# One core, a mixer kernel from a written-out order of 638 tasks: a new order on every engine

## The chip, the cores and the metric

The kernel runs on one core of a Trainium2 chip. The metric is the time of one execution on the device, in microseconds. The five engines are called by the names that the profile uses: PE (matrix products), DVE (vector), ACT (activation functions), POOL and SP. SP does no arithmetic here and only issues transfers; ACT and POOL issue a few as well.

## What is computed

```python
xn = _layernorm(x)                      # x: 1 x 2048 x 448
s = _A_ref(xn, ...)                     # h[t] = Lam_bar * h[t-1] + B_bar xn[t];  y = 2 Re(C h) + xn * Dskip
g = _silu(_B_ref(xn, ...))              # _layernorm, w1 (448 x 1792) + b1, gelu, w2 (1792 x 448) + b2
return x + s * g
```

The recurrence has 448 complex states with diagonal `Lam_bar = exp(dt * Lam)`. All inputs and the output are bf16.

## The kernel before

The 2048 rows are cut into four groups g of 512 rows, each group into two blocks b of 256 rows, each block into its even and odd rows (par 0 and 1), so that a tile has 128 partitions of 448 elements. The stages of a group are:

- the two layernorms at once: statistics of x (L378, for group 0 L399), scale factors (`ln_scale`, L440 to L450), and the application that writes `xn_sb` (for the recurrence) and `xn2_sb` (for the MLP; both show as `xn_sb` in the profile, L464 and L465, for group 0 L419);
- transposes of both to `xnT` and `xn2T`, for group 0's MLP operand on PE with copies by ACT and DVE (L422, L390), for all others by DMA transposes that SP issues (L83);
- the first MLP product, `mm1` (L741 and L742), seven pairs j of feature tiles, each in two phases, with a GELU on ACT for each pair (L745); a pair holds two PSUM banks until its GELU has read them, so that pair j=5 of a group can begin only after the GELU of pair j=2;
- the second, `mm2` (L760 and L762), with a bias addition on DVE (L763, it reads `b2bc`), a tanh on ACT (L764) and a gate on DVE (L765);
- the recurrence: `bu` (L669), a rotation and two scans on DVE (`ssm`, L684 to L715), and the output product `ym` (L793 to L799), after which DVE multiplies by the gate and adds the skip terms (L802, L805).

Tables are computed once from the parameters: sines on ACT into `WT` (L599; these need their own activation table, which is loaded before them, and GELU's table is loaded again after them, L604), products `LB` from B (`combine`, L619 to L622, an ACT or DVE half that writes `tmp` and a DVE half), their transposes `BT`, and `CQ`, `CZ` from C. `M0` (L658 to L660) is a product of these tables. The skip vector `dbc` and the bias `b2bc` are loaded by POOL, `dbc` only after `b2bc` has landed (L356 and L357); `dbc` is then halved by one small instruction (L359).

Nothing of the order is left to a scheduler at run time. The program adds 638 tasks, each with an engine, its instructions, and the names it reads and writes. `link` derives the dependences from the names in the order in which tasks were added. `ORDER` (L152) lists the task numbers in the order of issue, so that each engine gets its own tasks in the order in which the list names them, and `SECOND` (L171) lists the tasks, of those added with two possible engines, that run on the second one. Within an engine a waiting task holds up all that stand behind it; this holds for SP's queue of transfers too.

```python
        for k in SECOND:
            self.tasks[k].choose(1)
        order = [self.tasks[k] for k in ORDER]
...
        for t in order:
            eng, seen = self.engs[t.eng], self.seen[t.eng]
...
            for sem, val in need.items():
                if seen.get(sem, 0) < val:
                    eng.wait_ge(self.sems[sem], val)
                    seen[sem] = val
```

In the order before, SP loads block 1 of x first, then the even and the odd rows of block 0, then the pieces of w1, x of group 1, w2, C and B. The first DMA transpose in SP's queue is one of C (`Cr<-vs`, L83), which waits for the loads of C; behind it stand the two transposes `xn2T` of group 1's MLP operand, then x of group 2, and the transposes of group 0's `xnT`, of C and of B. PE runs 28 products on `ident` alone at the start (L829), which fill time only.

Of the kernel before, what the change touches and what calls it, by code (L numbers as in the profile page):

```python
# [149 lines left out]


ORDER = [int(k) for k in """  # L152
# [17 lines left out]
""".split()]  # L170
SECOND = [int(k) for k in """  # L171
23 34 45 65 66 73 75 78 80 82 84 85 89 100 132 156 158 160 184 186 191 195 219 221 225 241 245 247 248 257 261 265 267 323 324 325 326 334 346 355 363
374 375 385 396 400 402 443 444 446 469 483 484 501 503 504 506 507 508 509 515 517 528 532 533 616 632
""".split()]


# [748 lines left out]
```

## Time and profile before

| what | us |
|---|---|
| median of 3 runs (lowest to highest) | 158.9 (158.78 to 159.37) |
| profiled execution | 160.4 |
| its span, first to last instruction | 158.7 |
| PE busy | 148.0 (93%) |
| DVE busy | 136.2 (86%) |
| ACT busy | 96.6 (61%) |
| POOL busy | 38.9 (25%) |

The granted clock is 1.000 over the span. All times in a trace are counted from the span's start. Records of one engine overlap a little where one instruction follows another without a wait, so that their durations add up to more than the busy time; PE's overlap most, and for PE the distance from one group's start to the next's is used.

### The profile page before, as it was taken

How to read it: one execution, taken by the hardware profiler on the slowest of the kernel's cores; microseconds unless marked ns; L12 is line 12 of the kernel's file. 1: busy time of each engine (PE TensorE's matmuls, PEld its weight loads, DVE VectorE, ACT ScalarE, POOL GpSimd, SP SyncE). 2: the span in 40 equal slices, each digit the busy share in tenths (PEclk: the TensorE clock that was granted, in tenths of full speed). 3: DMA queues.
4: the chain of work that ended last, by engine and by line, in shares of the span. 5: the costliest groups of instructions: out<-in, count | busy, mean ns of one | idle time of the engine just before them, and what ended most of it. 6: DMA issues, size and time to landing. Idle time of an engine off the chain costs nothing.

```text
span 158.7 us, 3107 instructions
## 1 busy us (share of the span) xinstructions
PE 148.0 (93%) x1130; PEld 88.2 (56%) x1130; DVE 136.2 (86%) x295; ACT 96.6 (61%) x180; POOL 38.9 (25%) x94
## 2 busy tenths in 40 slices
PE   0989999499989999999999999999999999999992
PEld 0977755154446656665564555676444665555552
DVE  1789998379699799999899799857899978999794
ACT  3598978997599767597989251231484767035110
POOL 5628623030902000036000008450000260001231
PEclk9999999999999999999999999999999999999999
DMA  4999967999997450000000335310940000000103
GB/s 110 271 302 281 326 183 141 166 222 244 136 173 147 65 99 0 0 2 0 4 0 0 66 62 99 100 40 1 94 145 0 0 4 0 0 31 27 62 2 116
DMA packets 31238, 14.75 MB, mean 93 GB/s; under 512 B 24752, under 2 KB 30774, under 8 KB 31222
## 3 DMA queue, kind: packets, MB, share of 16 engines
q1 hardware_dynamic: 30912, 14.26, 41.7%
q0 software_dynamic: 160, 0.23, 1.0%
q8 instruction: 9, 0.15, 0.4%
q10 hardware_dynamic: 150, 0.05, 0.1%
q14 instruction: 7, 0.06, 0.1%
HBM read 6.89 MB, written 1.84 MB: 55 GB/s over the span
## 4 chain that ended last, share of the span: by engine, by line
PE 70%; DMA 14%; SPq 9%; DVE 2%; issue 2%; ACT 1%; DVEq 0%
PE psum L760 20%; PE psum L741 15%; PE psum L669 14%; PE psum L793 12%; DMA Bn<-in_A_B_im_dram 7%; SPq L84 7%; PE psum L796 4%; DMA x_all<-in_A_x_dram 4%; PE psum L658 3%; DMA xnT<-xn_sb 3%; SPq L83 2%; PE psum L799 1%; DVE lnst L378 1%; ACT gT L745 1%; ACT xn_sb L465 0%
## 5 line engine op out<-in xcount | busy, mean ns | idle before, releaser
L741 PE MATMUL psum<-xn2T,w_sb 64*128 64x512 bf16 (+1 forms) x462 | 45.5, 345 | 3.4 <-DMA xn2T<-xn_sb 2.4
L760 PE MATMUL psum<-w_sb,gT 128*128 128x448 bf16 x224 | 44.5, 353 | 0.0
L745 ACT ACTIVATE gT<-psum,b1f 128x512 bf16<-128x512 f32 (+1 forms) x66 | 36.1, 621 | 6.0 <-PE psum L741 5.6
L741 PEld LDWEIGHTS psum<-xn2T,w_sb 64*128 64x128 bf16 x462 | 25.5, 109 | 21.4 <-issue 5.3
L760 PEld LDWEIGHTS psum<-w_sb,gT 128*128 128x128 bf16 x224 | 21.6, 98 | 20.4 <-issue 0.6
L669 PE MATMUL psum<-xnT,BT 128*128 128x256 bf16 x196 | 24.1, 273 | 0.5 <-issue 0.5
L669 PEld LDWEIGHTS psum<-xnT,BT 128*128 128x128 bf16 x196 | 18.6, 98 | 6.5 <-issue 1.6
L390 ACT ACTIVATE u_sb<-psum 128x512 bf16<-128x512 f32 (+2 forms) x21 | 9.9, 470 | 14.1 <-PE psum L669 14.0
L764 ACT ACTIVATE th<-o 128x448 f32<-128x448 f32 x16 | 9.1, 576 | 9.7 <-DVE o L763 9.6
L390 ACT ACTIVATE vs<-s_w 64x256 bf16<-64x256 f32 (+2 forms) x14 | 7.9, 565 | 11.5 <-DVE s_w L695 7.5
L777 POOL TENSOR_TENSOR xr<-xd,g_sb 128x448 f32<-128x448 bf16 x4 | 4.8, 1194 | 41.1 <-DVE tmp L805 23.2
L693 DVE TENSOR_TENSOR_SCAN s_w<-dk,vs 128x774 f32<-128x774 f32 x8 | 13.9, 1758 | 0.0
L465 ACT ACTIVATE xn_sb<-x_all,lnw 128x448 bf16<-128x448 bf16 (+2 forms) x18 | 11.4, 672 | 3.9 <-POOL xd L777 2.2
L802 DVE TENSOR_TENSOR t<-psum,g_sb 128x448 bf16<-128x448 f32 (+2 forms) x17 | 10.0, 591 | 4.3 <-PE psum L796 2.3
L704 POOL TENSOR_TENSOR ang<-s_w,ang 128x16 f32<-128x16 f32 x3 | 2.0, 677 | 40.3 <-ACT s_w L702 20.7
L793 PE MATMUL psum<-CZ,h_sb 128*128 128x448 bf16 x56 | 11.9, 353 | 0.0
L763 DVE TENSOR_TENSOR o<-psum,b2bc 128x448 f32<-128x448 f32 x16 | 9.8, 615 | 1.0 <-PE psum L760 1.0
L765 DVE SCALAR_TENSOR_TENSOR g_sb<-th,o 128x448 bf16<-128x448 f32 x16 | 10.4, 650 | 0.2 <-ACT th L764 0.2
L793 PE MATMUL psum<-CQ,h_sb 128*128 128x448 bf16 (+2 forms) x54 | 10.5, 332 | 0.0
L378 DVE BATCH_NORM_STATS2 lnst<-x_all 128x6 f32<-128x448 bf16 x12 | 7.3, 619 | 1.4 <-DMA x_all<-in_A_x_dram 1.4
L619 ACT ACTIVATE tmp<-Cr,cw 128x448 f32<-128x448 bf16 (+1 forms) x10 | 6.5, 664 | 2.6 <-DVE CZ L622 1.3
L793 PEld LDWEIGHTS psum<-CZ,h_sb 128*128 128x128 bf16 x56 | 5.4, 98 | 4.9 <-DVE o L763 0.4
(161 smaller groups left out, 193.8 us busy)
## 6 DMA issues: line engine op xcount, KB each, us to landing
out_dram<-tmp SPq DMA_DIRECT2D x7, 224.0 KB, 1.9
x_all<-in_A_x_dram SPq DMA_DIRECT2D x3, 448.0 KB, 5.7
w_sb<-in_B_w_dram SPq DMA_DIRECT2D x3, 448.0 KB, 8.5
w_sb<-in_B_w_dram SPq DMA_DIRECT2D x3, 384.0 KB, 5.2
vs<-in_A_C_re_dram SPq DMA_DIRECT2D x1, 392.0 KB, 7.6
vs<-in_A_C_im_dram SPq DMA_DIRECT2D x1, 336.0 KB, 10.7
Bn<-in_A_B_re_dram SPq DMA_DIRECT2D x1, 336.0 KB, 11.0
Bn<-in_A_B_im_dram SPq DMA_DIRECT2D x1, 336.0 KB, 11.6
```

The lines of the kernel that those rows point to most:

```text
L84: return e.dma_start(out_ap, in_ap)
L390: kb.either(("act", [lambda e, o=o, i=i: e.activation(o, i, ACT.Copy) for o, i in pairs]), ("dve", [lambda e, o=o, i=i: e.tensor_copy(o, i ...
L465: ("act", [lambda e, o=o, i=i: e.activation(o, i, ACT.Identity, bias=nb, scale=rs) for o, i in parts], 0.75, 0.2)]
L669: fns = [lambda e, r=r, m=m, d=d: e.matmul(psum[:, 4, r * NK:(r + 1) * NK], BT[:, m, d, :], xnT[:, gx, d, :], start=(d == 0), stop=(d == 6 ...
L693: dve(lambda e, so=so, vi=vi: e.tensor_tensor_scan(so, dk[:].rearrange("p i c -> p (i c)"), vi, 0.0, ALU.mult, ALU.add), ["v", "vl", "dk", ...
L741: return lambda e: e.matmul(view(bk[k]), w1_sb[rows, d, fcol(2 * j + k)], rhs[rows, d, :, :], start=not second and n == 0, stop=second and ...
L745: act([lambda e, k=k: e.activation(gT[:, gb, 2 * j + k, :].rearrange("p (r c) -> p r c", r=2)[:, :, cols], view(bk[k]), ACT.Gelu_apprx_tan ...
L760: fns = [lambda e, fi=fi: e.matmul(psum[:, bk, 0:D], gT[:, gb, fi, q * 128:(q + 1) * 128], w2_sb[:, fi, :], start=(fi == 0), stop=(fi == N ...
L763: dve(lambda e: e.tensor_tensor(o2[:, fb, :], psum[:, bk, 0:D], b2bc[:], ALU.add), [f"ps{bk}", "b2bc"], [f"oo{fb}"], 0.62, prio - 76)
L765: dve(lambda e: e.scalar_tensor_tensor(out=g_sb[:, gs, :], in0=th[:, fb, :], scalar=1.0, in1=o2[:, fb, :], op0=ALU.add, op1=ALU.mult), [f" ...
L793: fns = [lambda e, k=k: e.matmul(psum[:, bk, c0:c1], h_sb[:, hb, k, k0:k0 + 128], cm[:, k, c0:c1], start=(k == 0), stop=False) for k in ra ...
L802: dve(lambda e: e.tensor_tensor(t3[:, fb, c0:c1], psum[:, bk, c0:c1], g_sb[:, gs, c0:c1], ALU.mult), [f"ps{bk}", f"g{gs}"], [f"t3{fb}_{c0} ...
```

## The change

Only the two lists change. The 638 tasks, what each computes, and the dependences between them stay. 77 of the tasks that may run on either of two engines now run on the other one: 25 go from DVE to POOL, 14 from DVE to ACT, 24 from ACT to DVE, 14 from POOL to DVE. PE and SP keep their 128 and 59 tasks. The places that matter below (a place is the position in the engine's own queue):

| task | what | before | after |
|---|---|---|---|
| 20, 18, 19 | loads of x: block 1, block 0 even rows, block 0 odd rows | SP 1st, 2nd, 3rd | SP 3rd, 2nd, 1st |
| 1, 90 | `ident` finished; the 28 filling products | POOL behind the b1 loads; PE behind the parameters | POOL ahead of the b1 loads; PE first |
| 213 | first transpose of C | SP 23rd | SP 29th |
| 260, 263 | `xn2T` transposes of group 1 | SP 24th, 25th | SP 21st, 22nd |
| 203 | load of the real part of C | SP 12th | SP 23rd, behind 263 |
| 257 | scale factors of group 1 | DVE | POOL, directly ahead of 43 |
| 43, 44 | loads of `b2bc` and `dbc` | POOL 30th, 41st | POOL 22nd, 27th |
| 259 | application, group 1, block 0, odd rows | DVE | ACT |
| 45 | halving of `dbc` | DVE | ACT 29th, ahead of the sines |
| 189 | `tmp` for the first `LB` | DVE | ACT 30th, ahead of the sines |
| 190 | first `LB` | DVE 59th | DVE 57th, behind both bias additions of group 0's block 0 |
| 278 | `mm2` of group 0, block 1, even rows | PE behind five phases of group 1's `mm1` | PE ahead of all of group 1's `mm1` |
| 315, 461, 457 | three `mm2` of groups 1 and 2 | PE 65th, 87th, 103rd | PE 83rd, 111th, 115th |
| 630, 634 | the last two output pieces | 256 columns, then 192 | 192 columns first; last addition on DVE |

The first lines of both lists, old and new:

```diff
 ORDER = [int(k) for k in """
-13 20 0 16 9 24 15 18 17 19 4 25 21 22 1 26 14 124 30 91 27 47 90 48 125 49 50 29 92 94 2 93 51 46 54 66 52 55 95 97 32 53 96 122 57 23 203 105 98 58
-101 99 205 123 106 100 102 103 126 5 104 33 56 39 108 107 40 112 130 42 28 114 59 65 113 127 41 109 60 154 38 111 110 128 204 131 129 115 35 117 37
-116 31 118 132 120 168 34 3 252 133 119 61 67 251 62 140 69 121 68 135 256 160 70 250 155 8 71 12 72 134 74 73 136 170 6 249 139 43 144 75 255 169 167
...
+0 5 16 19 13 9 1 90 24 15 25 18 94 14 95 20 91 4 21 92 105 22 26 17 96 47 101 124 93 27 97 122 102 48 65 106 23 125 99 29 50 98 30 100 123 2 49 51 54
+52 104 55 103 3 108 66 56 126 46 28 107 112 113 109 8 111 114 127 110 128 130 131 32 53 31 170 132 167 57 250 33 251 249 34 115 67 42 6 58 129 41 59
+117 140 116 118 10 133 254 40 168 252 119 120 121 135 144 139 134 136 255 256 253 12 39 141 137 60 257 145 142 43 169 154 62 7 171 258 149 146 63 74
...
 SECOND = [int(k) for k in """
-23 34 45 65 66 73 75 78 80 82 84 85 89 100 132 156 158 160 184 186 191 195 219 221 225 241 245 247 248 257 261 265 267 323 324 325 326 334 346 355 363
-374 375 385 396 400 402 443 444 446 469 483 484 501 503 504 506 507 508 509 515 517 528 532 533 616 632
+52 62 65 66 67 69 74 76 83 85 89 100 106 132 155 156 159 163 176 183 184 187 189 219 223 225 229 235 239 241 243 245 248 259 261 326 340 353 377 378
+396 443 444 447 468 469 480 481 484 500 506 508 510 513 528 636
```

28 rows, old and new, of the table ORDER are left out of this document.

## The prediction

> **What bounds the kernel now.** I read the page's chain first, then busy time by stretches cut at PE's own waits, then the timelines of the engines around those waits.
>
> ```profile
> PE 70%; DMA 14%; SPq 9%; DVE 2%; issue 2%; ACT 1%; DVEq 0%
> ```
>
> The chain that ended last is PE for 70% of the span. So every microsecond in which PE has nothing to do counts, and the stretches say where these are (columns: stretch, length, then busy time of PE, PEld, DVE, ACT, POOL).
>
> ```profile
> 0.79:9.06 8.27, 4.67 (x58) 4.40 (x59) 4.75 (x18) 4.25 (x12) 4.33 (x17) 1.00 0.86 216
> 9.06:20.98 11.92, 11.86 (x177) 9.33 (x178) 10.99 (x52) 10.98 (x23) 7.31 (x31) 1.00 1.09 307
> 20.98:29.08 8.10, 8.10 (x43) 4.00 (x42) 6.96 (x20) 6.40 (x12) 1.71 (x5) 1.00 0.83 132
> 29.08:31.45 2.37, 0.00 (x1) 0.03 (x1) 0.69 (x1) 2.36 (x3) 0.00 (x0) 1.00 0.75 184
> 31.45:45.23 13.78, 12.96 (x105) 6.54 (x105) 11.35 (x32) 10.93 (x19) 5.50 (x13) 1.00 1.17 201
> 45.23:155.19 109.96, 109.86 (x747) 63.58 (x748) 100.09 (x171) 61.70 (x115) 19.14 (x24) 1.00 0.21 42
> 155.19:158.70 3.51, 0.56 (x7) 0.34 (x5) 1.36 (x4) 0.00 (x0) 0.75 (x1) 1.00 0.39 131
> ```
>
> The first `mm1` begins at 9.06 (PE's busy time before it is mostly the 2.98 us of filling products). Then PE idles 2.37 us in one piece, 0.8 us up to 45.23, 0.1 us in the next 110 us, and it is done 3.5 us before the end. An order can move only these: 9.06, 2.37, 0.8 and 3.5. No PE instruction goes away.
>
> The 2.37 us are a wait for group 1's `xn2T`:
>
> ```profile
> 31.45 3.86 PE L741 MATMUL psum<-xn2T,w_sb 64*128 64x512 bf16 x34 [2.37 <-DMA xn2T<-xn_sb]
> ```
>
> and SP's queue shows why it was late: the transpose of C stands in front (22.56, it waits for C's loads), and a load of 448 KB right behind.
>
> ```profile
> 22.56 1.59 SPq L83 DMA_TRANSPOSE Cr<-vs  x1
> 24.20 2.68 SPq L83 DMA_TRANSPOSE xn2T<-xn_sb  x2
> 26.93 0.72 SPq L84 DMA_DIRECT2D x_all<-in_A_x_dram  x1
> ```
>
> **Start.** Before, block 0's odd rows were the third load; DVE's statistics on them began at 5.43, and the chain statistics, Ln and Exp, application (7.01), transpose (7.82), copy on ACT (8.25 to 8.85) led to 9.06. Loaded first, the odd rows should land 2.4 to 3.0 us after 0.79 (rows of the 112 KB loads), so this part ends two microseconds earlier. But DVE's new queue has block 1's first statistics ahead of the application of block 0's even rows, and block 1, now third, lands at about 5.4. From there: statistics 0.54, application to 6.4, transpose to 7.1, then DVE must do block 1's second statistics, the b1 copy and the w1 copy (moved to it from ACT) before the last copy, 7.4 to 7.8. `mm1` starts near 7.9. Block 1's own factors (1.54 us on DVE) then begin at about 8.2, just where they were (8.09), but the two applications follow sooner; its transposes come at about 10.5 where they were at 11.36. From there PE is full to 20.98. I take **-0.8**; the ends are -0.2 (the factors decide alone) and -1.1.
>
> **The wait for `xn2T` goes: -2.37.** Group 1's scale factors, 20.28 before, are on POOL now: 3.5 us (row of group 2's, 39.33 to 42.87) after the sine's 3.2 us, which I place at 11.5 to 14.7; so 18.3. The applications, two of four on ACT behind group 0's GELUs, end near 21 and 23, and SP issues the transposes at about 21.5 and 23 instead of 24.20 and 25.54. Moreover `mm2` of 278 (2.65 us) now stands ahead of group 1's `mm1`. PE asks for `xn2T` at 31.0: 20.2 plus 8.1 plus 2.65. Even with the 5.8 us that the second transpose took before, it is there by 29.
>
> **What is late next: the GELUs of group 1.** ACT's new queue has, behind group 0's last GELU (about 25), the halving of `dbc`, then `tmp` of the first `LB`, then the sine stage. The halving was on DVE at 33.16 with nobody behind it in a hurry; now ACT stands until `dbc` has landed. POOL issues `dbc` only when `b2bc` has landed, and `b2bc` only behind the scale factors, at 18.3 instead of 16.24. Both landings have rows:
>
> ```profile
> b2bc<-in_B_b_dram POOLq DMA_DIRECT2D x1, 112.0 KB, 6.5
> dbc<-in_A_Dskip_dram POOLq DMA_DIRECT2D x1, 112.0 KB, 5.3
> ```
>
> The smallest POOL loads took 2.9 and 3.4. I take 5.0 for `b2bc` (fewer loads are ahead of it than at 16.24) and 5.2 for `dbc`: landing at 28.5, between 24.1 (twice 2.9) and 31.3 (twice 6.5). Then ACT needs: halving 0.6 (no row; 0.26 on DVE below, 0.76 for an ACT application of that size above), `tmp` 0.6, and the sine stage,
>
> ```profile
> 26.92 1.28 ACT L599 ACT_TABLE_LOAD   x1
> 28.21 1.72 ACT L599 ACTIVATE WT<-s_w 128x768 bf16<-128x768 f32 x2
> 29.84 0.65 ACT L619 ACTIVATE tmp<-Bn,cw 128x448 f32<-128x448 bf16 x1
> 30.40 2.21 ACT L599 ACTIVATE WT<-s_w,sgn 128x1024 bf16<-128x1024 f32 x3
> 32.69 1.28 ACT L604 ACT_TABLE_LOAD   x1
> ```
>
> from 26.92 to 33.97 less the `tmp` in it, 6.5; then a tanh 0.5 and the first pair of GELUs 1.1: 9.3, so 37.8. PE reaches pair j=5, which needs these banks, at 31.0 plus five phases 3.8 plus one 0.85, 35.6. It waits 2.2, and 0.5 more for j=3, whose GELU pair ends 1.17 later: **+2.7**. The same wait holds `LB` on DVE (190 needs that `tmp`), hence `BT` and `bu`.
>
> [...]
>
> **The rest.** The 0.8 us of small idle: BT's transposes still come one per 1.3 us from SP and follow `LB`; I keep 0.5, **-0.3**. In the 110 full microseconds DVE's records give up 18.7 us and take 15.8 (by the rows of the forms they become), so its load is not higher; the three late `mm2` fill PE between `ym` pieces. I set it at 0, between 0 and +2. Tail: before, the last 192 columns waited for DVE until 156.38 and their load-out was issued at 156.78; now these are finished first, and the last piece ends with a multiplication 0.43 and an addition (0.75 on POOL before, some 0.4 on DVE): **-0.5**, ends 0 and -0.7.
>
> **Sum** against the span of 158.7: -0.8 -2.37 +2.7 -0.3 +0 -0.5 = -1.3. The profiled execution took 160.4, 1.7 outside the span; the median of the runs shown is 158.9, from which the same -1.3 gives **157.6**.
>
> **Rivals.**
> - *POOL's loads land early.* If `dbc` is there by 26.3, the GELUs are no later than PE and the 2.7 go: 154.9. For: fewer transfers run at 18 to 25. Against: both rows above.
> - *`dbc` lands late and ACT's wait outweighs all.* Slower than before from a landing after 29.8, by over 0.5% after 30.6. With scale factors one microsecond later and 6.5 for each load: 32.3, so 161.4. For: the load's packets moved only at 21 to 22, five microseconds after 16.24, and the same POOL operation (L578, 128x128) took 0.49 in one place and 0.65 in another. [...]
> - *Handovers between DVE and PE.* DVE's queue is strict, and PE now meets it closely: the bias addition behind 315, the second `ym` of each block waiting for the multiplication that frees its bank, `CZ` for the first `ym`. Five such waits of 0.4 (the size of the small waits at 43.9 and 45.2) make 2: 159.4 or so.
> - *Nothing net:* the new wait equals all gains, 158.9.
>
> **How the numbers follow.** Forecast 157.6 with its own range 156.9 to 158.1: 0.42. Early loads 154.9: 0.15. Late `dbc` 161.4: 0.20. Handovers 159.4: 0.15. Nothing net: 0.08. A measurement of this kernel can tell about 0.5%, 0.8 us. Faster 0.57, within 0.23, slower 0.20. The range goes from 154.9 to 160.2: all but the far part of the late case.
>
> **What would show it.** `mm1` near 7.9; no wait for `xn2T`; a wait of ACT for `dbc`, ending near 28.5, and one of PE for GELUs of 2 to 3 us at 36 to 39. Without ACT's wait the sum is wrong by 2.7. If PE idles by more than 1 us in sum after 45, DVE's handovers were mis-sized.

## The result and the profile after

The changed kernel takes 163.7 us (median of 4, 163.14 to 165.81), the kernel before 159.1 beside it: **1.027 times as long**, interval 1.022 to 1.032. The forecast was 157.6, so not only the size but the sign was wrong.

The first profiled execution of the changed kernel took 165.8 us, with the granted clock at 0.979: it fell to half in two stretches of 3.4 us. So the times below are from a second profiled execution of the same kernel (after_again, below): 164.8 us, span 163.0, clock 1.000, against 160.4 and 158.7 before.

The page's chain now reads as follows. It was PE for 70% before, and DVE for 2%.

```profile
DVE 48%; PE 25%; DMA 10%; issue 6%; POOL 5%; SPq 2%; ACT 2%; DVEq 0%; POOLq 0%; ACTq 0%
```

Busy time by stretches of after_again, cut at the start of `mm1`, the end of group 0's `mm1`, PE's wait for GELUs at 38, the first `bu` and PE's end (columns as before: stretch, length, PE, PEld, DVE, ACT, POOL, then the granted clock, the DMA engines' share and GB/s):

```profile
9.09:22.63 13.54, 13.54 (x177) 10.58 (x178) 10.37 (x44) 10.24 (x23) 7.82 (x22) 1.00 0.81 242
22.63:37.99 15.36, 15.36 (x99) 7.67 (x98) 12.49 (x29) 12.06 (x21) 6.37 (x19) 1.00 0.89 155
37.99:39.08 1.09, 0.00 (x1) 0.01 (x2) 1.09 (x3) 1.09 (x3) 0.96 (x4) 1.00 1.00 196
39.08:43.47 4.39, 3.98 (x34) 2.16 (x35) 3.86 (x11) 4.12 (x8) 0.00 (x0) 1.00 0.96 114
43.47:159.44 115.97, 112.65 (x767) 64.64 (x765) 107.81 (x181) 58.11 (x108) 33.80 (x47) 1.00 0.23 51
159.44:163.00 3.56, 0.00 (x0) 0.00 (x0) 1.56 (x5) 0.00 (x0) 0.57 (x1) 1.00 0.38 129
```

The wait for `xn2T` is gone. But the 177 products and transposes of group 0's `mm1`, which took 11.92 us, take 13.54; PE waits 1.1 us at 38; PE is idle for 3.3 us of the long stretch, where it was 0.1; DVE is busy for 93% of it, where it was 91%; and the tail is 3.56 instead of 2.91 (from PE's last product). What PE waits for, from the view of waits (total, times, longest); of the first row 1.5 us lie at 38 to 40.3, before the long stretch:

```profile
PE psum L741 <- ACT gT L745: 2.0, 3, 1.1
...
PE psum L793 <- DVE t L802: 1.4, 1, 1.4
PE psum L669 <- ACT u_sb L390: 1.0, 1, 1.0
```

Between the two profiled executions the span grew by 4.3 us: group 0's `mm1` +1.6, PE's waits behind it +1.4 (3.2 to 4.6), the tail +0.65, and the rest in waits below 0.2 us and in the interleaving of PE's work. The first of these terms belongs to these two executions: over the profiles of all runs, group 0's `mm1` ends at 20.4 to 22.7 with the start of the changed kernel (nine profiles, the middle one 21.6) and at 21.0 to 23.2 with that of the kernel before (seven, the middle one 21.5).

### The profile page after: what moved, and what is told of

The parts are those of the page before. It is cut to its first block, busy times and chain, and to the rows that moved or that the text cites. A ratio compares the mean times of both kernels' runs of the same rounds, so it can differ in the third digit from the quotient of the medians.

```text
span 164.1 us, 3109 instructions
## 1 busy us (share of the span) xinstructions
PE 151.4 (92%) x1130; PEld 89.2 (54%) x1130; DVE 142.5 (87%) x285; ACT 89.8 (55%) x168; POOL 54.0 (33%) x111
## 4 chain that ended last, share of the span: by engine, by line
DVE 43%; PE 28%; ACT 8%; DMA 7%; issue 6%; POOL 5%; DVEq 0%; ACTq 0%; POOLq 0%
PE psum L741 14%; DVE s_w L693 5%; PE psum L793 5%; DVE t L802 4%; DVE tmp L805 4%; DVE g_sb L765 4%; DVE lnst L378 3%; PE psum L760 3%; DMA dbc<-in_A_Dskip_dram 3%; PE psum L669 3%; ACT WT L599 2%; POOL lnw L442 2%; DMA dk<-in_B_b_dram 2%; DVE o L763 2%; DVE CZ L622 2%
## 5 line engine op out<-in xcount | busy, mean ns | idle before, releaser
L741 PE MATMUL psum<-xn2T,w_sb 64*128 64x512 bf16 (+1 forms) x462 | 48.1, 363 | 3.0 <-ACT gT L745 2.5
L741 PEld LDWEIGHTS psum<-xn2T,w_sb 64*128 64x128 bf16 x462 | 26.9, 112 | 22.9 <-issue 4.8
L390 ACT ACTIVATE u_sb<-psum 128x512 bf16<-128x512 f32 (+2 forms) x20 | 10.0, 498 | 22.3 <-PE psum L669 22.2
L777 POOL TENSOR_TENSOR xr<-xd,g_sb 128x448 f32<-128x448 bf16 x6 | 6.9, 1153 | 24.8 <-DVE g_sb L765 15.6
L802 DVE TENSOR_TENSOR t<-psum,g_sb 128x448 bf16<-128x448 f32 (+2 forms) x17 | 9.9, 593 | 3.9 <-PE psum L796 3.0
L464 DVE TENSOR_SCALAR xn_sb<-x_all,lnw 128x448 bf16<-128x448 bf16 (+2 forms) x25 | 10.7, 452 | 1.7 <-ACT xn_sb L465 0.8
L465 ACT ACTIVATE xn_sb<-x_all,lnw 128x448 bf16<-128x448 bf16 (+2 forms) x15 | 9.0, 646 | 3.4 <-POOL lnw L444 3.3
L765 DVE SCALAR_TENSOR_TENSOR g_sb<-th,o 128x448 bf16<-128x448 f32 x16 | 9.7, 619 | 1.1 <-ACT th L764 1.1
L777 POOL TENSOR_TENSOR xr<-x_all,xr 128x448 f32<-128x448 bf16 x6 | 7.6, 1259 | 5.1 <-DVE xr L778 4.9
L704 POOL TENSOR_TENSOR ang<-s_w,ang 128x16 f32<-128x16 f32 x2 | 0.5, 242 | 25.6 <-ACT s_w L702 25.6
```

The lines of the kernel that those rows point to most:

```text
L390: kb.either(("act", [lambda e, o=o, i=i: e.activation(o, i, ACT.Copy) for o, i in pairs]), ("dve", [lambda e, o=o, i=i: e.tensor_copy(o, i ...
L464: on = [("dve", [lambda e, o=o, i=i: e.tensor_scalar(o, i, rs, nb, op0=ALU.mult, op1=ALU.add) for o, i in parts], 0.4, 0.12), ("act", [lam ...
L741: return lambda e: e.matmul(view(bk[k]), w1_sb[rows, d, fcol(2 * j + k)], rhs[rows, d, :, :], start=not second and n == 0, stop=second and ...
L765: dve(lambda e: e.scalar_tensor_tensor(out=g_sb[:, gs, :], in0=th[:, fb, :], scalar=1.0, in1=o2[:, fb, :], op0=ALU.add, op1=ALU.mult), [f" ...
L777: kb.either(("pool", lambda e, o=o, i0=i0, i1=i1, op=op: e.tensor_tensor(o, i0, i1, op), 1.37, 0.15), ("dve", lambda e, o=o, i0=i0, i1=i1, ...
L802: dve(lambda e: e.tensor_tensor(t3[:, fb, c0:c1], psum[:, bk, c0:c1], g_sb[:, gs, c0:c1], ALU.mult), [f"ps{bk}", f"g{gs}"], [f"t3{fb}_{c0} ...
```

## The experiments

All are compared with runs of the kernel before on the same chip (159.4 to 159.6 us). Theory G: the late `dbc` and the wait for GELUs is what the change lost. Theory D: DVE has become the bound after 45 us, stretched by POOL's work. A third, the clock theory, came with the first profiles.

| run | us | ratio to before, interval |
|---|---|---|
| old45_new | 163.5 | 1.023, 1.018 to 1.029 |
| new45_old | 168.4 | 1.057, 1.053 to 1.062 |
| bias_early | 164.8 | 1.036, 1.031 to 1.041 |
| skips_dve | 165.2 | 1.037, 1.033 to 1.042 |
| after_again | 164.1 | 1.030, 1.025 to 1.035 |
| fill42 | 164.6 | 1.029, 1.023 to 1.035 |
| pool_tiny | 160.5 | 1.007, 1.004 to 1.010 |
| before_xt | 163.1 | 1.023, 1.017 to 1.028 |
| before_tiny | 161.5 | 1.013, 1.008 to 1.019 |
| after_act | 171.6 | 1.079, 1.073 to 1.085 |
| act_start | 171.0 | 1.075, 1.069 to 1.080 |
| before_xt2 | 159.6 | 1.002, 0.998 to 1.005 |
| stats_cut | 162.9 | 1.022, 1.018 to 1.026 |
| before_double | 164.2 | 1.028, 1.024 to 1.032 |
| tiny_start | 158.1 | 0.993, 0.990 to 0.997 |
| before_xt3 | 159.7 | 1.001, 0.998 to 1.003 |
| gelu_early | 163.2 | 1.024, 1.018 to 1.030 |
| gelu_fill | 161.2 | 1.011, 1.005 to 1.017 |

### Halves of the two orders

```diff
-ORDER = NEW
+ORDER = OLD[:280] + [k for k in NEW if k not in OLD[:280]]
```

> Every engine follows the old order for what it issues up to about 45 us and the new one from there, with the new choice of engines for that part. Theory G (the late dbc, PE's wait for GELUs at 37, is what the change lost, and the rest only hands it on): nothing of it is in this kernel, so about the time before, 158.5 to 159.5. Theory D (DVE has become the bound after 45: in the changed kernel's profile it has 104.8 us of work left after 50 us, before 96.8, and its operations that run beside POOL's are stretched by 8.8 us in sum, before 3.1): 161 to 162.5, with PE waiting for DVE or ACT between 60 and 115.

```diff
-ORDER = NEW
+ORDER = NEW[:270] + [k for k in OLD if k not in NEW[:270]]
```

> The other half: every engine follows the new order up to about 45 us and the old one from there. Theory G: PE's wait for GELUs (2.0 us in the profiled execution, 3.7 where the clock is not lowered before it) is in this kernel, no wait for xn2T; 161.5 to 163. Theory D: the gains of the start and of xn2T against that wait leave about +1, 159.5 to 160.5.

(`SECOND` follows the order in each part.) The first is slow, by 1 us more than D's range allowed, with the 1.4 us wait for L802 at 110 and no loss ahead of 45. The second is slower than either order and than both expectations: PE waits 5.7 us at 53.3 for ACT's copy of `u_sb`, a wait that neither order has. A joint of two orders makes waits of its own, so these two say only that the late part is slow by itself.

### The filling products and the clock

```diff
-... start=True, stop=True) for _ in range(28)],
+... start=True, stop=True) for _ in range(42)],
```

> The changed kernel itself, on the chip of the three that follow, for a base to compare them with and for another profile of it. 163 to 164.5. If DVE is what bounds it after 45, its profile shows PE waiting again near 65, 81 and 111, whatever the clock at 8 and at 39 did.

> The changed kernel with 42 filling products instead of 28, so that PE is busy from 1.7 to about 6.4 instead of to 4.9. Clock theory (the filling products end too early, PE stands 1.5 us, and the next 3.4 us run at half rate): the first 14 mm1 products should take 0.33 to 0.45 us a phase again instead of 0.6 to 0.85, and PE should be 1.5 us further at 12 us. At the end: -1.5 if PE bounds what follows; about 0 to -0.4 if PE only asks earlier for the GELUs at 35 to 39 and later for DVE (theory D).

PE's timeline at the start of after_again,

```profile
1.74 3.17 PE L829 MATMUL psum<-ident 128*128 128x128 bf16 x28 [1.74 <-POOL ident L298]
...
9.09 4.35 PE L741 MATMUL psum<-xn2T,w_sb 64*128 64x256 bf16 x40 [0.19 <-DVE cw L529]
```

and of fill42:

```profile
1.73 3.81 PE L829 MATMUL psum<-ident 128*128 128x128 bf16 x42 [1.73 <-POOL ident L298]
...
8.40 2.38 PE L741 MATMUL psum<-xn2T,w_sb 64*128 64x256 bf16 x40 [0.48 <-DVE cw L529]
```

28 filling products take 3.17 us, one per 0.107 us in the trace. The 42 take 3.81, because from 4.5 us on there is one per 0.056. So PE begins at half rate here, and when it goes to full rate differs: 2.8 us after its first product in fill42, and in gelu_fill not within the 4.66 us that the same 42 take there. In after_again the filling ends at half rate, PE then waits 1.5 us for the bias columns, and the same 40 products of `mm1` take 4.35 us instead of 2.38. The granted clock reads 1.00 in both (each microsecond from 9 to 13); the spacing of the products is what shows it. In the changed kernel's first profile it went another way: PE was at full rate at 6.8 (four of the transposes in 0.40 us, 0.61 in after_again), and the granted clock was 0.50 from 8.4 to 11.8. With 28 products in the new place these 40 take from 2.38 (after_act) to 4.35 us in nine profiles, with 42 always 2.38 (four profiles). In that first profile the half clock lasted 3.4 us both times (8.4 to 11.8, 39.1 to 42.5). What decides between the rates no run here shows.

fill42 is 2.2 us further at the end of group 0's `mm1` (20.41 against 22.56, the starts of `mm2`) and in the median not faster at the end: PE reaches the GELUs sooner, waits there for 1.4 and 0.4 us, and then the clock is at 0.50 from 38.6 to 42.0, so that 28 products take 4.90 us (3.22 in after_again):

```profile
38.53 4.90 PE L741 MATMUL psum<-xn2T,w_sb 64*128 64x512 bf16 x28 [0.41 <-ACT gT L745]
```

Four of its six executions have a mean clock of 0.985 to 0.987 like this one; the two at 1.000 took 162.6 and 162.9 us, over 1 us less than after_again. So what the added products gained was lost again to the wait and, in most executions, to the clock behind it.

### The wait for the GELUs

In these and the next, POOL's queue is shown as task numbers.

```diff
-12 60 257 43 7 63 64 158 44
+12 43 60 44 257 7 63 64 158
```

> The changed kernel with b2bc's load moved in POOL's queue to 10.6 us (where POOL has nothing to do) and dbc's load ahead of group 1's scale factors. dbc should land near 22 instead of 29.1, ACT should not wait for it, and the GELU that PE waits for should end near 35.3 instead of 39.0. Theory G: the wait goes and the time with it, 160 to 160.5. Theory D: PE asks earlier and waits later for DVE instead; no more than 1.5 us of it shows at the end, 162.2 to 163.5.

It did not test what it was to test: `b2bc`, issued at 12.4, took 6.8 us in the crowd of the first loads (347 GB/s in that slice of the page), POOL stood 2.7 us for it ahead of group 1's scale factors, and what stood behind them came 2 to 3 us later. So the factors go first:

```diff
-12 60 257 43 7 63 64 158 44
+12 43 60 257 44 7 63 64 158
```

> The changed kernel with b2bc's load as soon as POOL is free for it (about 12.5) and dbc's right behind group 1's scale factors; nothing is left out. bias_early tried this and failed to test it, since POOL waited for b2bc ahead of the scale factors and all behind them came 3 us late; here the factors go first. ACT should not wait for dbc, and the GELUs that PE waits for at 37 to 39 should end 2 us sooner or more (36.3 in tiny_start). Theory G: PE's wait falls below 0.5 us and 1.5 to 3 us come back, 161 to 162.5. Theory D: the wait goes and little shows at the end, 163 to 164.5.

> gelu_early with 42 filling products: both losses ahead of 45 us undone, the skip products whole and beside DVE as in the changed kernel. tiny_start, the same with cut skip products, took 158.1. Theory D: 161.5 to 163.5, some 4 to 5 us above tiny_start, with PE waiting near 65, 81 and 111. If the losses ahead of 45 us were the cause: 158.5 to 160.5.

In gelu_early `dbc` lands at 24.9 and ACT doesn't wait; PE's waits for GELUs fall from 2.0 to 0.5 us (a new one of 0.5 for a transpose of `BT` follows), and 0.6% come back, 1.0 us (the two intervals, 1.018 to 1.030 and 1.025 to 1.035, overlap). Both losses ahead of 45 undone (gelu_fill) bring 1.9%, 3.0 us, though the filling products alone brought nothing. Neither loss shows fully while the other is there: PE that is early waits for the GELUs, and GELUs that are early wait for a late PE. In gelu_fill the mean clock is 0.996 or more in every execution, so what fill42 lost to the clock is not lost there. Theory D alone expected 161.5 or more, theory G alone 160.5 or less; 161.2 lies between them, nearer to D.

### POOL's skip products beside DVE

```diff
-SECOND = NEW_SECOND
+SECOND = NEW_SECOND + {247 323 324 325 363 507 509 616}
```

> The changed kernel with the eight skip products that went from DVE to POOL (1.0 to 1.7 us each there, 0.38 to 0.62 on DVE before) back on DVE, at the same places of the order. Theory G: they lie beside other work, 163.2 to 164.2. Theory D in the form that POOL's work stretches DVE's: 4.5 us come back to DVE and about as much stretching goes, 162 to 164, with the stretched DVE operations at 60 to 63 and at 136 back to 0.4 to 0.95 us. If it is clearly slower than 164.2, the moves to POOL were worth more than the stretching they cost.

```diff
-... ("pool", lambda ...: e.tensor_tensor(o, i0, i1, op), ...)
+... ("pool", lambda ...: e.tensor_tensor(o[:, 0:8], i0[:, 0:8], i1[:, 0:8], op), ...)
```

> The changed kernel with every skip product on POOL (L777) cut to 8 of its 448 columns, so the output lacks most of the skip term in those places; all waits stay, and POOL's busy time falls from 54 to about 33 us. Theory D with stretching (DVE's operations beside POOL's take 8.8 us longer in sum, most of it beside these products): DVE's busy time falls by 4 to 5 us, the wait at 111 (1.4 us) goes, the end comes 2.5 to 4 us earlier, 160 to 161. If the stretching is only beside the point, 163 to 164.

(pool_tiny, before_tiny and tiny_start also clear `xd` and `xr` once, 1.7 us on POOL in its idle time.) DVE's timeline of after_again ahead of PE's longest wait for DVE,

```profile
107.00 1.31 DVE L464 TENSOR_SCALAR xn_sb<-x_all,lnw 128x384 bf16<-128x384 bf16 x2
108.23 0.61 DVE L805 TENSOR_TENSOR tmp<-t,xr 128x448 bf16<-128x448 bf16 x1
108.77 1.78 DVE L685 TENSOR_TENSOR pb<-u_sb,WT 128x1536 bf16<-128x1536 bf16 x1
110.48 0.38 DVE L805 TENSOR_TENSOR tmp<-t,x_all 128x448 bf16<-128x448 bf16 x1
110.89 0.62 DVE L802 TENSOR_TENSOR t<-psum,g_sb 128x448 bf16<-128x448 f32 x1
```

POOL's at the same time,

```profile
107.11 1.15 POOL L777 TENSOR_TENSOR xr<-xd,g_sb 128x448 f32<-128x448 bf16 x1
108.34 1.40 POOL L777 TENSOR_TENSOR xd<-xn_sb,dbc 128x448 bf16<-128x448 bf16 x1
109.69 0.94 POOL L709 COPY h_sb<-h_sb 128x7 bf16<-128x7 bf16 x1
```

and DVE's in pool_tiny, where those products are cut:

```profile
104.93 0.60 DVE L464 TENSOR_SCALAR xn_sb<-x_all,lnw 128x384 bf16<-128x384 bf16 x2
105.45 0.62 DVE L805 TENSOR_TENSOR tmp<-t,xr 128x448 bf16<-128x448 bf16 x1
105.98 0.95 DVE L685 TENSOR_TENSOR pb<-u_sb,WT 128x1536 bf16<-128x1536 bf16 x1
```

The same two DVE rows take 1.31 and 1.78 us beside POOL, 0.60 and 0.95 without, and POOL's small copy (0.21 before) takes 0.94. The 1.5 us in these two rows is what makes the multiplication of L802 late, for which PE stands 1.38 us; in pool_tiny that wait is not there. From the first `bu` to PE's last product, PE is idle for 0.06 us in pool_tiny (length less PE's busy time), where it was 3.3 in after_again and 0.1 before:

```profile
43.70:155.74 112.04, 111.98 (x767) 65.03 (x765) 100.98 (x183) 58.09 (x108) 18.98 (x43) 1.00 0.23 54
```

It is not that POOL's products themselves are late: in after_again neither DVE, ACT nor PE waits for one. Over the whole kernel, the DVE operations that overlap POOL's are 8.4 us longer than their own kind elsewhere (before 3.1, pool_tiny 1.8), and the cut gives back 3.6 us. Moving the eight tasks back to DVE (skips_dve) halves the stretching to 4.3 but gives DVE its work again: DVE is busy for 142.1 us, as in the changed kernel, and nothing is won (165.2 against 164.1 us, with overlapping intervals).

L802, which reads PSUM, keeps its length: its two at 156.19 take 1.15 us together beside a POOL product of 1.11, and in the first profile its operations on 448 columns take at most 0.63 each, the six beside POOL's work as well. So in these rows L685 and L464 are held up and L802 is not. POOL's products are stretched too: the one at 108.34, which began 0.11 us behind a DVE addition (L805, 0.61 as elsewhere), took 1.40, where the one at 29.89 took 1.03. Why some operations are held up and others not is not shown.

Two controls (before_tiny with pool_tiny's edit on the kernel before), and the opposite experiment on the kernel before:

> A control for the cut skip products: the kernel before with every skip product on POOL cut to 8 of 448 columns (most of the skip term is lacking where POOL computes it). There DVE's operations beside POOL's are stretched by 3.1 us in sum, and PE has 0.1 us of idle time from 45 on. Theory D: PE bounds this kernel, so what DVE gets back is not worth anything: 158.5 to 159.5, against -3.6 us in the changed kernel. If cut skip products make any kernel faster (fewer waits on POOL), it gains 1.5 us or more here as well.

```diff
-e.bn_stats(lnst[:, q, :], x_all[:, 2 * g + b, par, :])
+e.bn_stats(lnst[:, q, :], x_all[:, 2 * g + b, par, 0:(D if g < 2 else 16)])
```

> The changed kernel with the eight statistics of groups 2 and 3 (L378 on DVE, 0.61 us each) taken over 16 of 448 columns, so the layernorm of half of the rows is not the reference's. Order, queues and POOL's work stay; DVE has some 3.7 us less to do between 51 and 90 us. If DVE is the bound there, 1.5 to 3.5 us come back: 160.5 to 162.5. If it is not, and only POOL's products themselves were late in pool_tiny: 163.5 to 164.5.

```diff
-("pool", lambda ...: e.tensor_tensor(o, i0, i1, op), ...)
+("pool", [lambda ...: e.tensor_tensor(o, i0, i1, op)] * 2, ...)
```

> The kernel before with each of its eleven skip products on POOL done twice (where that product adds x, x is added twice). POOL gets some 12 us more, still under 35% busy. Stretching: about half of a POOL product's length is added to DVE's operations beside it, so DVE's sum of stretching goes from 3.1 to 6 or more, and the time, where DVE has little room left, by 1 to 4 us: 160.5 to 163. If POOL beside DVE costs nothing in this order: 159 to 160.

before_tiny missed its range: in its profile PE stayed at half rate until 13.3, and group 0's `mm1` ended at 23.2 instead of 20.98, so its sum is no clean control; three of its six executions also have a mean clock of 0.987 to 0.989. From the first `bu` to the end it takes 113.5 us, the kernel before 113.4; pool_tiny takes 115.1 there and after_again 119.5 (in the changed order 14 products of `mm1`, 1.6 us, lie behind the first `bu` that lay ahead of it before). So the cut is worth 4.4 us in the changed order and nothing in the old one. stats_cut takes 3.5 us off DVE's busy time with POOL untouched and is 0.8%, 1.3 us, faster than after_again, between its two ranges and with intervals that just touch: DVE's work counts there, at about a third of its length. before_double shows the same from the other side: added POOL work alone, in the old order, takes DVE from 136.2 to 142.2 busy, the stretching from 3.1 to 9.2, PE's idle time behind the first `bu` from 0.1 to 3.1,

```profile
42.96:157.32 114.36, 111.30 (x751) 63.52 (x751) 106.40 (x176) 61.31 (x115) 32.56 (x37) 1.00 0.20 41
```

and the time to 1.028, which is what the whole change did and more than its range. A part of that is waiting for the longer products themselves (DVE stands 0.9 us at 96.2 for one, ACT 5.5 for another, 2.2 before), so of the two the cut is the cleaner experiment.

tiny_start has the edits of pool_tiny, fill42 and gelu_early:

> pool_tiny (skip products on POOL cut to 8 columns, 160.5) with 42 filling products and b2bc loaded at about 12 and dbc right behind group 1's scale factors, which should bring dbc to about 25.5 instead of 29 and the GELUs 3 us forward. If the changed kernel's gains at the start were hidden behind DVE, they should show now that DVE has room: 157.5 to 159. If the order loses them again in any case (another wait between 45 and 110), 160 to 161.

0.993 (0.990 to 0.997): with the skip products cut, the earlier start and GELUs show, and only then is the new order faster than the old, by 1.1 us, though it lacks work.

### Less work on DVE by way of ACT

```diff
-SECOND = NEW_SECOND
+SECOND = NEW_SECOND - {229 235 239 243 340 377 378 480 481 513} + {446 501 503 504}
```

> The changed kernel with 14 of the 24 tasks that went from ACT to DVE back on ACT, all those after 50 us, at the same places of the order. DVE loses about 8.6 us of work after 50 us (103.8 of it in the changed kernel, 96.8 before), ACT gains 12. Theory D: DVE is the bound there, so 2 to 4 us come back, 160 to 162. If order and not load is what makes it slow, or ACT's queue now holds GELUs up: 163.5 or more.

act_start adds the edits of bias_early and fill42, moves 217 and 218 in SP's queue behind 165 and 206 (without their wait for `Ct0`), the eight statistics tasks of group 2 behind 196 on DVE and 373 behind 79 on POOL:

> after_act and, on top, 42 filling products, the early b2bc and dbc, and the loads of groups 2 and 3 of x, the statistics and scale factors of group 2 at 28 to 42 us instead of 47 to 60. Theory D: once DVE has less to do late, the earlier start (PE 2.9 us further at 20 us with 42 filling products) and the GELUs that come sooner count: 157 to 159.5, near or below the kernel before. If DVE bounds it still, no better than after_act.

Both fell far: DVE has 94.6 us of work after 50 us in after_act, less than before, and the time is 171.6. PE waits 2.9 us at 59.6 for a copy of `u_sb` that ACT has behind an application given to it, and 3.7 at 126.6 for a transpose `xnT`, which SP could issue only at 127.3, behind another application on ACT. So the load of DVE is no measure by itself: in queues this strict, a task put back without a new order costs more than it frees. Theory D as "so many microseconds on DVE" fell with it; what stands is that operations made longer in place delay PE.

### The wait for xn2T alone

SP's queue:

```diff
-37 213 260 263 217 165
+37 260 263 213 217 165
```

> The kernel before with one part of the change alone: SP issues the first transpose of C and the load behind it after the two transposes of group 1's xn2T instead of ahead of them. The xn2T transposes should be issued at 21.5 to 23.5 and PE's wait of 2.37 us at 29 go. If the wait was worth what it lasts: 156.5 to 157. If the next wait takes its place (GELUs of group 1, which end at 35.8 and 37.6 because the sines end at 34, and the transposes of BT, which SP issues in turn): 158 to 159, with PE waiting at 37 and ahead of the first bu.

Here 217 stands behind 213, since it waits for it. The wait at 29 falls from 2.4 to below 0.2 us, and the kernel is 2.3% slower: PE waits 0.6 us at 38 and 1.9 at 42.7 for GELUs, the latter behind an application on ACT that waits for a transpose now later in SP's queue, and behind these waits the clock is at 0.50 from 45.4 to 48.9. Neither expectation named this wait. Next, 217 and 218 without their wait for the transpose of C (`Ct0`), SP's queue with 166 sooner, and ACT's with the two applications behind the GELUs:

```diff
-37 213 260 263 217 165 215 214 218 206 209 166 216
+37 260 263 217 213 165 166 215 214 218 206 209 216
-289 265 295 272 292 267 298 304 301
+289 295 265 272 292 298 304 301 267
```

> The kernel before with the xn2T transposes and the load of group 2 ahead of the first transpose of C, the second xnT transpose of group 0 sooner, and two applications on ACT put behind the GELUs that they held up. The one-part kernel lost 3.6 us: PE waited 1.9 us at 42.7 for GELUs behind an application that waited for that xnT transpose, 0.6 us at 38, and ran 3.4 us at half clock after 45.4. If those waits are the whole reason, 157 to 158.5; if PE then waits for BT's transposes ahead of the first bu, 158.5 to 160; with the clock at half again, 161 or more.

```diff
-206 209 216 36 207 208
+206 207 209 216 36 208
```

> before_xt2 with the second BT transpose that the first bu needs moved in SP's queue ahead of two other transposes. In before_xt2 (equal to the kernel before) PE still waited 1.2 us for it at 43.6. If that wait is the last one in its way: 158 to 158.7, a version faster than both; if the next transposes or DVE are late in turn: 159 to 160.

Both equal the kernel before. In before_xt2 PE waits 1.2 us at 29.6 for `xn2T` and 1.2 at 43.6 for a transpose of `BT`; in before_xt3 the first is 0.9 us, the second is gone, and no gain can be measured. Where those 1.2 us went in its median execution stays open: its profiled execution, 158.8 us, is one of its two fastest.

## Why the prediction was wrong

**The start, -0.8.** The odd rows landed at 2.86, and `mm1` did begin sooner in the first profile (8.51, forecast 7.9; 9.09 in after_again). But the forecast held the filling products for padding ("PE's busy time before it is mostly the 2.98 us of filling products") and gave their move no price. They end at 4.9 instead of 7.1, PE waits behind them, and a part of `mm1` runs at half rate (its first 40 products take 3.96 us in the first profile and 4.35 in after_again, 2.37 before): group 0's `mm1` ends 0.6 us (first profile) or 1.6 us (after_again) later than in the profile of before, instead of 0.8 earlier. With 42 filling products it ends at 20.4 in fill42, near the forecast's 20.2.

**The wait for `xn2T`, -2.37.** Right as an event: the transposes were issued at 22.3 and 24.0 (forecast 21.5 and 23), landed by 29.3, and PE asked at 32.3.

```profile
22.34 2.85 SPq L83 DMA_TRANSPOSE xn2T<-xn_sb  x2
25.23 0.58 SPq L84 DMA_DIRECT2D vs<-in_A_C_re_dram  x1
```

That is the first profile of the changed kernel; the load of C that stood ahead of them is behind them now. As a term of a sum it was wrong: with this wait alone taken away the kernel is 3.6 us slower (before_xt), and with the next waits taken away as well the time is as before. The step that added up 2.37 as a gain looked at what follows only as far as the GELUs.

**The wait for GELUs, +2.7.** Right in mechanism, and nearly in size with some luck. `dbc` landed at 29.07 in the first profile (forecast 28.5): the scale factors ended at 20.4 instead of 18.3, `b2bc` then took 3.5 us instead of 5.0 and `dbc` 5.0 instead of 5.2, so that two errors of about 2 us cancelled. ACT in after_again:

```profile
29.17 0.58 ACT L358 ACTIVATE dbc<-dbc 128x448 bf16<-128x448 bf16 x1 [2.73 <-DMA dbc<-in_A_Dskip_dram]
...
30.32 1.28 ACT L599 ACT_TABLE_LOAD   x1
...
37.77 3.56 ACT L745 ACTIVATE gT<-psum,b1f 128x512 bf16<-128x512 f32 x6
```

The pair that PE needs ended at 39.0 (forecast 37.8), and PE, late from the start, waited 2.0 us in all in after_again and 2.5 in the first profile. Undone alone it gives back 1.0 us; with the start, 3.0. The measured 3.5 and 5.0 for the two loads (3.2 and 4.3 in after_again) are below the rows of before, 6.5 and 5.3.

**The small idle, -0.3.** About right: PE's 0.34 and 0.48 us before the first `bu` became one wait of 0.41 for a GELU, and PE does not wait for `BT`.

**45 to 155 us, 0: the step that failed most.** The forecast said that "DVE's records give up 18.7 us and take 15.8", and from that, "so its load is not higher". Both figures are sums over the whole kernel and not over the 110 us: of the 18.7 only 11.8 lie behind 45.23, and as much is taken there. Measured over the whole kernel (first profile), the tasks moved give up 18.7 and take 17.2, and **the tasks that stayed on DVE take 5.9 us longer**, 141.1 for 135.3: POOL's busy time went from 38.9 to 54.0, and DVE's operations beside it were stretched (by 8.8 us in sum, 3.1 before). A duration was carried from a row in which POOL was idle to a place where it isn't. pool_tiny prices it at 3.6 us, gelu_fill against tiny_start at 2.8. The forecast had named the sign, more than 1 us of PE idle after 45; it was 3.3.

**The tail, -0.5.** It became +0.65. The reordered last pieces find DVE late, beside POOL's last skip product:

```profile
157.78 1.23 DVE L805 TENSOR_TENSOR tmp<-t,x_all 128x448 bf16<-128x448 bf16 x1
```

That addition took 0.38 before; PE's last product now lies 1.6 us ahead of the last load-out's issue, where it lay 1.0. With the skip products cut (pool_tiny) the tail is 3.09 instead of 3.56.

**The rivals.** The late-`dbc` rival had the right sign and a wrong cause: it decides from a landing after 29.8, and `dbc` landed at 29.1. The handover rival (159.4) had the right place, and five waits of 0.4 us for a cost of 3 to 4.

By ratios: start and GELUs together 1.030 to 1.011, the skip products beside DVE 1.011 to 0.993, and the gains, last of all, 0.7%. Open is how much of before_xt3's vanished wait lies in the state of the clock at the start, and why the half clock hardly ever showed in the kernel before, with its wait of 2.4 us at 29 (2 of some 80 executions have a mean clock of 0.989, the others 0.997 or more), while before_xt, with its 1.9 us at 42.7, has a mean clock of 0.989 in 5 of 6.

## What to carry to other kernels

A task moved to POOL isn't gone from DVE: price it by the DVE operations that will run beside it (here up to 0.9 us longer each, L684 with 1.80 us for 0.95), and not by the row it had alone. A wait that is removed is worth what the next wait leaves of it, so follow PE to the next three things it will ask for, and never add up waits as gains. Work that only fills PE's time isn't free to move: here the first 40 products of `mm1` took 2.38 to 4.35 us behind 28 filling products in the new place (4.35 in after_again) and 2.38 behind 42 (fill42), so look at the spacing of the first real products before and after such a move.

## What the runs showed of the hardware

PE's first products run at half rate in nine profiles (before, both of the changed kernel, skips_dve, fill42, gelu_fill, before_tiny, before_xt2, before_double), 0.107 us for a 128x128 product against 0.056, while the granted clock reads 1.00 (before, 4.0 to 7.2; first profile of the changed kernel, 1.5 to 8.0). When they go to full rate differs from one execution to the next, from 6.8 us in the kernel before (the first 40 products of `mm1` in 2.37 us) to 13.3 in before_tiny (in 4.06), whose starts have the same 28 filling products. A wait of PE of 2.0 us (first profile, 37.0 to 39.0), one of 1.9 (before_xt, 42.7 to 44.6) and one of 1.4 with 0.4 behind it (fill42, then 28 products in 4.90 us for 3.22) were each followed by 3.4 us at a granted clock of 0.50; behind the wait of 2.37 in the profile of before it read 1.00 from 31 to 35. A POOL product made DVE operations beside it up to 0.9 us longer (first profile: 1.80 for 0.95 in L684 at 136.38, beside a product of L777 that began at 135.68; 1.78 for 0.95 in L685 at 109.84), left L685 at 135.51 as it was (0.95, with that product beginning 0.17 us behind it), and was itself stretched, from 1.03 to 1.68 there and to as much as 1.75 elsewhere. And a load of 112 KB issued by POOL took 6.8 us at 12.4 (bias_early, 347 GB/s in that slice of the page), 6.5 at 16.2 (before, 326 GB/s), 3.5 at 20.4 (first profile, 83 GB/s in the slice from 20.5) and 3.2 at 21.3 (after_again, 34 GB/s).
